# Last slot weights in a buffer part of their own, turned ahead of the last two experts; one cast of the slot outputs; output in eight transfers

## The chip, the cores and the metric

One core of one Trainium2 chip runs the whole program. The time is the device time of one execution in microseconds (us). An execution that was profiled has a span as well: from its first instruction to its last, as the trace shows it.

## What is computed

The first half is a linear attention with a decaying state over 4 batches, 8 heads, 768 steps and head width 48. Its output, seen as 3072 tokens of 384 values, goes into a soft mixture of experts: 8 experts with 4 slots each, so 32 slots.

```python
x = attn_out.transpose(0, 2, 1, 3).reshape(B * S, H * D)   # 3072 x 384
logits = x @ phi                                           # 3072 x 32
d = softmax of logits over the tokens;  slot_input = d.T @ x
for e in range(8):
    slot_out[e] = relu(slot_input[e] @ w1[e]) @ w2[e]      # 4x384, 384x1024, 1024x384
c = softmax of logits over the slots
out = c @ slot_out                                         # 3072x32 @ 32x384
```

The change touches only the end: the weights c of the last tokens ("slot weights"), the second product of the experts, and the product c @ slot_out with the transfers of its result.

## The kernel before, in words

The program is written as named tasks (`add(name, engines, function, ...)`), and the string `ORDER` (lines 9 to 32) lists the tasks in the order in which they are issued. Each engine works through its own instructions in that order; a word such as `ND3:ACT` puts a task on the named engine. Engines wait for each other through semaphores, which the framework sets from the tiles and the parts of tiles that instructions read and write. Tiles come from named pools and go back to them when their last task is issued.

Attention runs in 12 units, and behind each three units the logits of a batch are worked on. The token axis is cut into pieces: three batches whole (pieces 0 to 2), then batch 3 in a piece of four chunks of 128 tokens (piece 3) and one of two chunks (piece 4, the last). For a piece b, the slot weights go through these tasks:

- `LT`, `SU`, `LC`, `NM` (lines 670 to 710): logits, minus their maximum over the slots, exponential, sum and reciprocal, in the tile `Ls` (float32).
- `NB` (line 713): `Ls` times the reciprocal, written as bf16 into the tile `Lc`, on POOL for pieces 0 and 1 and on DVE (VectorE) otherwise.
- `ND` (line 725): a copy inside `Lc` that repeats part of each group of 32 columns; on POOL unless the word in `ORDER` says otherwise.
- `LX` (line 766): PE (TensorE) turns `Lc`, one 128x128 transpose per chunk, into a PSUM tile.
- `LE` (line 770, recorded at the helper's lines 358 for DVE and 360 for ACT): the turned weights go to `LexpT`, slots by tokens.

`Lc` and `Ls` have room for six chunks, and there is one tile of each (lines 169 and 171): pieces use chunk places 0 to 3 (piece 3) and 0 to 1 (piece 4), so piece 4 writes where piece 3 was.

The experts' weights are loaded by tasks `W0` to `W15`, issued from POOL's queue, with a cast to bf16 on the way (lines 784 to 787). The last one, for the second matrix of the last expert, is cut into `W15a`, `W15b` and `W15`: four, three and one of its eight blocks. The second product of experts 4 to 7 is done by `Q10` (experts 4 and 5, 16 products), `Q11` (expert 6, 8), `Q12`, `Q13` and `Q14` (expert 7; 4, 3 and 1 products, each behind the load of its own blocks), line 923. All add up in one PSUM bank, `SO` (half of the tile `Yb`). `F` words are products whose result nobody reads (line 862); `F19_2` stands between `LX3` and `Q11`.

Behind the last task come lines 930 to 957: `SO` is cast to bf16 into `so`, the left half by ACT (ScalarE) and the right half by DVE. Then 24 rows follow: row i is the product of every 24th column of `LexpT`, starting at i, with `so` (line 951), whose 128x384 result is copied from PSUM by ACT for even i and by DVE for odd i (lines 953 and 955). Row 0 alone is made in two halves, one copied by each engine. After 1, 3, 4, 4, 4, 4 and 4 rows SP issues a transfer to the output (line 957). Each partition's rows lie side by side in the output, so a transfer of n rows moves one run of n x 1536 bytes per partition. The results wait in tiles that are free by then: `vT_all`, four parts of `mix`, one of the `raw` pool, `AT_all`.

Of the kernel before, what the change touches and what calls it, by code (L numbers as in the profile page):

```python
# [26 lines left out]
RM2 NM1 XE100:ACT EX2 W13 W14 NB1 L3 AL2 ET2 YE11 AC1 ZT2 RM3 EE2 ZC3 EX3 SU2 F10a_3 X111 X110 XE111:ACT AL3 F11a_1  # L27
ET3 W15a ND1 XE110 EE3:ACT LB4 RM4 DP2 G1 DP3 AC2 EX4 G2 ET4 AL4 G3 G5 LC2 GS EE4 F12_3 DP4 AC3 ZT3 AC4 LX1 NM2 NB2
F13a_1 MG UN SU3 LC3 F14_6 H00 R00:DVE NM3 H01 R01 F15a_5 HT00 ND2 W15b HT01 HE00 F16a_1 Q00 HE01 Q01 H11 LX2 LE2
R11 F17_2 LT4 H10 NB3 LE1:ACT R10:DVE SU4 W15 LC4 F18_6 HT11 HT10 HE10 HE11:ACT NM4 Q10 ND3:ACT LX3 NB4 F19_2 Q11  # L30
Q12 ND4 LX4 Q13 LE3 LE4 Q14
"""


# [12 lines left out]
class _Plan:  # L47
# [7 lines left out]
    def buf(self, pool):  # L55
        return _Buf(pool)

    def add(self, name, engs, fn, deps=(), bufs=()):
        self.by[name] = _Task(name, engs, fn, list(deps), list(bufs))
# [23 lines left out]
def kernel(  # L83
# [12 lines left out]
    nc = tc.nc  # L96
    B, H, S, D = r.shape
    C = 128
    NS = S // C
    Nn, Dm = out.shape  # L100
    ES = moe_phi.shape[1]
    E = moe_w1.shape[0]
# [17 lines left out]
    f32 = mybir.dt.float32  # L120
# [6 lines left out]
    def O(ins):  # L127
        return tc.keep_in_program_order(ins)

    pe, dve, act, pool, sp = nc.tensor, nc.vector, nc.scalar, nc.gpsimd, nc.sync  # L130
# [18 lines left out]
    vT_all = big.tile([128, 3 * HW], bf, name="vT_all")  # L149
# [9 lines left out]
    SW = nQ * D  # L159
    S_t = [cst.tile([128, nQ, 2, D], bf, name=f"S{j}") for j in range(3)]  # L160
    Z_t = [cst.tile([128, nQ, 2, D], bf, name=f"Z{j}") for j in range(3)]
    XW = Dm + 8
    x_t = [cst.tile([128, NS, XW], bf, name=f"x{j}") for j in range(NX)]
# [3 lines left out]
    xT_t = [xT_all[:, CC * j:CC * (j + 1)] for j in range(NXT)]  # L167
    LexpT = cst.tile([128, Nn], bf, name="LexpT")
    Lc_t = [cst.tile([128, NS, 128], bf, name=f"Lc{j}") for j in range(1)]
    zc_t = [cst.tile([128, 2 * C], f32, name=f"zc{j}") for j in range(1)]  # L170
    Ls_t = [cst.tile([128, NS, ES], f32, name=f"Ls{j}") for j in range(1)]
    E_t = [cst.tile([128, 2 * C], bf, name=f"E{j}") for j in range(2)]
    ET_t = [cst.tile([128, 2 * C], bf, name=f"ET{j}") for j in range(2)]
# [9 lines left out]
    T_t = [psb.tile([128, 1024], bf, name=f"T{j}") for j in range(3)]  # L183
    Ab = psb.tile([128, 2, 512], f32, name="Ab")
    Yb = psb.tile([128, 2, 512], f32, name="Yb")
    Y_t = [Yb[:, j, :] for j in range(2)]
    Mb = psb.tile([128, 512], f32, name="Mb")
# [157 lines left out]
    def consts_d():  # L345
# [4 lines left out]

    L = _Plan(dict(raw=raw, ks=ks_t, vj=vj_t, kn=kn_t, vn=vn_t, AT=AT_t, prs=pr_t[0:1], prl=pr_t[1:2], dv=dv_t,
                   **{f"{x}T": t for x, t in turned.items()},
                   S=S_t, Z=Z_t, x=x_t, zc=zc_t, Lc=Lc_t, Ls=Ls_t, E=E_t, ET=ET_t, T=T_t, A=[Ab], Y=[Yb], M=[Mb], **{f"xT{j}": [t] for j, t in enumerate(xT_t)}))
    buf, add = L.buf, L.add

    def ev(t, dst, src):
# [47 lines left out]
    for m in range(NLD):  # L404
        lg = m % 2
        pb = TT["p", m] = buf("pr" + "sl"[lg])
        for nm in "krv":
            dstT = TT[nm, m] = buf(nm + "sl"[lg] + "T")
            P = P2 if nm == "v" else 128
            for h in range(1 + lg):  # L410
# [3 lines left out]
                def rv(kb=kr[nm, m], lg=lg, h=h):  # L414
                    return rows(*kb, J if lg else JH)[:, :, h * JH:(h + 1) * JH]
# [6 lines left out]
                else:  # L422
# [3 lines left out]
                    def f_src(t, rv=rv, src=src, tab=tab):  # L426
                        eng = dve if t.eng == "DVE" else pool
                        O(eng.tensor_mul(src.inst.rearrange("p (j e s) -> p e j s", j=JH, e=2)[:, :, :, 0:D], rv(), tab))  # L428
                    sd = f"S{nm}{m}{hx}"
                    add(sd, "DVE" if m == 0 else "POOL DVE" if m < 2 else "POOL", f_src,  # L430
# [35 lines left out]
    for n in range(NU):  # L466
# [51 lines left out]
        Smid = buf("Z")  # L518
        Snew = Sb[n] = buf("S") if ui < U3 - 1 else None
        dvb = buf("dv")  # L520
# [42 lines left out]
        def f_y(t, Yf=Yf, rT=rT, vn=vn, dvb=dvb, Sold=Sold, Smid=Smid, a=tuple(ATb), n=n):  # L563
# [11 lines left out]
            for x in range(PH):  # L575
                q, c = cell(n, x)
                if c:
                    S = (Sold, Smid)[x // nQ]
                    O(pe.matmul(y[:, x // nQ, q * P2:(q + 1) * P2], rT.inst[:, x, :],  # L579
# [33 lines left out]
    for b, (bt, c0, c1) in enumerate(pieces):  # L613
        xb = xB[bt]
        nc_ = c1 - c0
        last = b == NPC - 1
        ny = 2 if nc_ == NS else 1
        us = list(range(U3 * bt + c0 // CC, U3 * bt + c1 // CC))
        xTs = [xTB[i] for i in us]
        Lcb, Lsb, Eb, ETb = buf("Lc"), buf("Ls"), buf("E"), buf("ET")  # L620
        nm_o, nm_n = nm_t[(b + 1) % 2], nm_t[b % 2]
        rm, al, mx, sm = rm_t[b % 2], al_t[b % 2], mx_t[b % 2], sm_t[b % 2]

# [183 lines left out]
    SX, SO = Y_t[0], Y_t[1][:, 0:Dm]  # L807
# [4 lines left out]
    so = cst.tile([128, Dm], bf, name="so")  # L812
# [105 lines left out]
    for name, g, prod, deps in parts:  # L918
# [8 lines left out]
        qd = name  # L927

    L.run(ORDER)
    O(act.copy(so[:, 0:Dm // 2], SO[:, 0:Dm // 2]))  # L930
    O(dve.tensor_copy(so[:, Dm // 2:Dm], SO[:, Dm // 2:Dm]))


    out_v = out.rearrange("(p n) m -> p n m", n=nN)
    ob = [T_t[0][:].bitcast(f32), T_t[1][:].bitcast(f32), T_t[2][:].bitcast(f32), Mb[:], Ab[:, 0, :], SX]
    mf = mix[:].bitcast(f32)
    OW = 4 * Dm
    obuf = [vT_all[:].bitcast(f32)] + [mf[:, x * OW:(x + 1) * OW] for x in range(4)] + [
        L.pools["raw"][0], AT_all[:].rearrange("p a b -> p (a b)").bitcast(f32)]
    sizes = [1, 3, 4, 4, 4, 4, 4]  # L940
    i = 0
    for gi, sz in enumerate(sizes):
        o_s = obuf[gi][:, 0:sz * Dm].rearrange("p (n m) -> p n m", m=Dm)
# [44 lines left out]
```

## Time and profile before

| | |
|---|---|
| runs | 120.91, 120.58, 119.62 us; median 120.58 |
| the profiled execution | 119.91 us, of which the span is 118.1 us |
| busy over the span | PE 98.4, DVE 94.2, ACT 86.4, POOL 62.1 us |
| moved by DMA | 31.81 MB; HBM read 39.42 MB, written 4.72 MB |
| granted TensorE clock, mean | 0.972 |

Times in the views are counted from the start of the span. A row of the timeline gives start, duration, engine, line, operation, tiles with shapes, count, and in brackets the idle time ahead of it with what ended it. The chain of work that ended last gives start, duration and the engine and line that the end hung on at that time; "issue" there is time in which nothing visible was waited for. A row of a table of windows gives the busy time of the engines (with counts), then the granted TensorE clock, the busy share of the 16 DMA engines and the GB/s that they moved. PE's rows are its products, PEld's the loading of their weights, and a Q after an engine's name is its sequencer or queue.

### The profile page before, as it was taken

Reading aid. Unit: us, or ns where it says so; the run is one execution under the profiler, and the core shown is the slowest. Engines: PE = TensorE matmul, PEld = TensorE weight load, DVE = VectorE, ACT = ScalarE, POOL = GpSimd, SP = SyncE. Lnnn points to the kernel's source line nnn. Section 1 sums busy time; section 2 is a strip of 40 time slices with the busy share of each in tenths; the row PEclk is TensorE's granted clock in tenths of the full one; section 3 lists DMA queues with packets and bytes.
Section 4 is the critical chain, followed back from the end, with each engine's and each line's share of the span. In section 5 each row is a group of like instructions: output and inputs, shape, how many; then the busy total and the mean of one; then the engine's idle time right before and its main releaser. Section 6 shows DMA issues by size and latency. Waiting matters only on the chain.

```text
span 118.1 us, 3926 instructions
## 1 busy us (share of the span) xinstructions
PE 98.4 (83%) x1657; PEld 71.9 (61%) x1662; DVE 94.2 (80%) x181; ACT 86.4 (73%) x139; POOL 62.1 (53%) x81
## 2 busy tenths in 40 slices
PE   3999895999999899897999998999889887795000
PEld 0366674788888788686778877877543443463000
DVE  6798987798999999798999989999889426499000
ACT  5759994999999999698899979979951243296000
POOL 7605999999999989999989210000505000000000
PEclk9999999999999999999999999999999999999855
DMA  1999999999999999999999999999999997149993
GB/s 31 315 375 389 392 400 398 381 394 397 381 382 373 316 230 222 214 218 212 214 216 218 209 221 212 214 218 208 222 210 221 209 209 132 20 193 419 416 410 160
DMA packets 10697, 31.81 MB, mean 269 GB/s; under 512 B 1336, under 2 KB 4664, under 8 KB 10680
## 3 DMA queue, kind: packets, MB, share of 16 engines
q0 software_dynamic: 2592, 12.58, 52.1%
q1 hardware_dynamic: 7944, 18.93, 42.5%
q8 instruction: 13, 0.21, 0.7%
q10 hardware_dynamic: 144, 0.05, 0.2%
q14 instruction: 4, 0.03, 0.1%
HBM read 39.42 MB, written 4.72 MB: 374 GB/s over the span
## 4 chain that ended last, share of the span: by engine, by line
PE 44%; DVE 25%; ACT 9%; POOL 7%; issue 6%; ACTq 1%; DVEq 1%; POOLq 0%
PE T L437 9%; POOL mix L428 6%; DVE AT_all L512 5%; PE Ab L507 4%; PE Yb L573 3%; DVE mix L955 3%; PE Yb L923 3%; PE Yb L568 3%; PE Yb L579 2%; PE T L482 2%; PE T L596 2%; PE T L492 2%; PE Mb L530 2%; PE Mb L533 2%; DVE dv L556 2%
## 5 line engine op out<-in xcount | busy, mean ns | idle before, releaser
L428 POOL TENSOR_TENSOR mix<-raw,tabl 128x768 bf16<-128x768 f32 x15 | 28.0, 1878 | 5.5 <-ACT tabl L398 5.4
L512 DVE TENSOR_TENSOR AT_all<-Ab,mask 128x1024 bf16<-128x1024 f32 x24 | 29.3, 1219 | 1.1 <-PE Ab L507 0.5
L360 ACT COPY mix<-T 128x1024 bf16<-128x1024 bf16 x19 | 19.1, 1021 | 4.9 <-PE T L437 3.4
L437 PEld LDWEIGHTS <-mix 128*128 128x128 bf16 x192 | 12.3, 101 | 2.4 <-DVE mix L428 0.7
L556 DVE TENSOR_TENSOR dv<-vn,Mb 128x768 bf16<-128x768 bf16 x12 | 11.4, 946 | 1.4 <-PE Mb L546 1.1
L428 POOL TENSOR_TENSOR mix<-raw,tabs 128x768 bf16<-128x768 f32 x6 | 10.8, 1816 | 0.0
L360 ACT COPY vT_all<-T 96x1024 bf16<-96x1024 bf16 x10 | 10.2, 1021 | 0.6 <-PE T L437 0.4
L507 PE MATMUL Ab<-mix 64*128 64x128 bf16 x192 | 9.5, 218 | 1.2 <-ACT mix L360 1.0
L360 ACT COPY xT_all<-T 128x768 bf16<-128x768 bf16 (+1 forms) x12 | 9.3, 784 | 1.3 <-PE T L596 1.3
L360 ACT CAST x<-Yb 128x768 bf16<-128x768 f32 x12 | 9.7, 807 | 0.1
L437 PE MATMUL T<-turnl,mix 128*128 128x128 bf16 x128 | 9.6, 219 | 0.1
L725 POOL COPY Lc<-Lc 128x384 bf16<-128x384 bf16 (+1 forms) x4 | 1.8, 460 | 14.5 <-DVE Lc L713 14.5
L713 POOL TENSOR_TENSOR Lc<-Ls,sm 128x192 bf16<-128x192 f32 x2 | 1.0, 504 | 15.0 <-ACT E L691 14.5
L360 ACT COPY vn<-T 128x768 bf16<-128x768 bf16 x11 | 8.8, 814 | 0.0
L453 DVE TENSOR_TENSOR pr<-T,mix 128x1024 bf16<-128x1024 bf16 x12 | 8.0, 683 | 0.0
L507 PEld LDWEIGHTS <-mix 64*128 64x128 bf16 x192 | 5.8, 94 | 3.5 <-issue 0.7
L573 PEld LDWEIGHTS <-AT_all 128*128 128x128 bf16 x192 | 6.7, 96 | 1.7 <-issue 0.2
L540 DVE TENSOR_TENSOR Z<-Mb,wT 128x384 bf16<-128x384 f32 x12 | 6.6, 553 | 0.9 <-PE Mb L533 0.8
L360 ACT COPY kn<-T 128x768 bf16<-128x768 bf16 (+1 forms) x10 | 7.2, 721 | 0.2
L573 PE MATMUL Yb<-vn,AT_all 128*128 128x48 bf16 x192 | 6.9, 183 | 0.1
L419 POOL CAST vj<-raw 128x768 bf16<-128x768 f32 x8 | 6.6, 830 | 0.6 <-POOL phi_s L337 0.6
L437 PEld LDWEIGHTS <-vj 128*96 128x96 bf16 x96 | 6.3, 123 | 1.0 <-issue 0.4
(187 smaller groups left out, 241.3 us busy)
## 6 DMA issues: line engine op xcount, KB each, us to landing
raw<-in_moe_w_dram POOLq DMA_DIRECT2D x13, 768.0 KB, 14.6
raw<-in_k_dram SPq DMA_DIRECT2D x4, 768.0 KB, 12.3
raw<-in_r_dram SPq DMA_DIRECT2D x4, 768.0 KB, 11.6
raw<-in_v_dram SPq DMA_DIRECT2D x4, 768.0 KB, 12.4
out_dram<-mix SPq DMA_DIRECT2D x3, 768.0 KB, 4.9
raw<-in_k_dram SPq DMA_DIRECT2D x4, 384.0 KB, 10.7
raw<-in_r_dram SPq DMA_DIRECT2D x4, 384.0 KB, 10.3
raw<-in_v_dram SPq DMA_DIRECT2D x4, 384.0 KB, 10.4
```

The source lines that it names most:

```text
L360: O(act.copy(dst, src))
L419: O(act.copy(o, i_) if t.eng == "ACT" else pool.tensor_copy(o, i_))
L428: O(eng.tensor_mul(src.inst.rearrange("p (j e s) -> p e j s", j=JH, e=2)[:, :, :, 0:D], rv(), tab))
L437: O(pe.transpose(Tb.inst[0:P, jj * 128:(jj + 1) * 128], sv[:, jj, :], (turn, turnl)[lg][:]))
L453: O(dve.tensor_mul(cv(pb), tv(), cv(kT)))
L507: O(pe.matmul(Abf.inst[:, e, x * C:(x + 1) * C], kT.inst[s, g * nQ + x, :], rT.inst[s, g * nQ + x, :]))
L512: O(dve.tensor_mul(AT.inst[:], Abf.inst[:].rearrange("p e (g t) -> p e g t", g=nQ), mask[:, None, None, :].to_broadcast([128, 2, nQ, C])))
L540: O(dve.tensor_mul(Smid.inst[:], Mf.inst[:, 0:SW].rearrange("p (q d) -> p q d", q=nQ)[:, :, None, :].to_broadcast([128, nQ, 2, D]), wT[:, ...
L556: O(dve.tensor_mul(dvb.inst[:].rearrange("p g e d -> p (g e) d"), vn.inst[:].rearrange("p g e d -> p (g e) d"), Mf.inst[:, 448:448 + 2 * P ...
L568: O(pe.matmul(y[:, h, 0:Dm], ident[:], dvb.inst[:, h * nQ:(h + 1) * nQ].rearrange("p g e d -> p (g e d)"), start=True, stop=False, skip_gr ...
L573: O(pe.matmul(y[:, x // nQ, q * P2 + e * D:q * P2 + (e + 1) * D], a[x // nQ].inst[:, e, q, :], vn.inst[:, x, e, :], start=False, stop=(c = ...
L923: O(pe.matmul(SO[32 * z:32 * z + 32, :], hT[g].rearrange("p y c -> p (y c)")[:, c:c + 32], w2_of(g * EG + x)[:, y, :], start=(g == 0 and y ...
```

## The change

- The last piece takes its `Lc` and `Ls` from pools of their own, `Lcl` and `Lsl`, which are chunk places 4 and 5 of the same tiles.
- In `ORDER`, `NB4` and `ND4` move ahead of `Q10`, and `ND4` runs on DVE, where it was on POOL behind `Q12`; `LX4` moves from behind `Q12` to right behind `LX3`; `F19_2` is gone; `LE3` moves ahead of `Q13`, and `LE4` runs on ACT in place of DVE.
- One ACT instruction casts all of `so`.
- The output goes in eight transfers of 1, 2, 3, 4, 4, 4, 4 and 2 rows. The second waits in `vT_all` beside the first; those behind it use the tiles as before, one transfer later.

```diff
-R11 F17_2 LT4 H10 NB3 LE1:ACT R10:DVE SU4 W15 LC4 F18_6 HT11 HT10 HE10 HE11:ACT NM4 Q10 ND3:ACT LX3 NB4 F19_2 Q11
-Q12 ND4 LX4 Q13 LE3 LE4 Q14
+R11 F17_2 LT4 H10 NB3 LE1:ACT R10:DVE SU4 W15 LC4 F18_6 HT11 HT10 HE10 HE11:ACT NM4 NB4 ND4:DVE Q10 ND3:ACT LX3 LX4
+Q11 Q12 LE3 Q13 LE4:ACT Q14
...
-                   S=S_t, Z=Z_t, x=x_t, zc=zc_t, Lc=Lc_t, Ls=Ls_t, E=E_t, ET=ET_t, T=T_t, A=[Ab], Y=[Yb], M=[Mb], **{f"xT{j}": [t] for j, t in enumerate(xT_t)}))
+                   S=S_t, Z=Z_t, x=x_t, zc=zc_t, Lc=Lc_t, Lcl=[Lc_t[0][:, NS - 2:]], Lsl=[Ls_t[0][:, NS - 2:]], Ls=Ls_t, E=E_t, ET=ET_t, T=T_t, A=[Ab], Y=[Yb], M=[Mb], **{f"xT{j}": [t] for j, t in enumerate(xT_t)}))
...
-        Lcb, Lsb, Eb, ETb = buf("Lc"), buf("Ls"), buf("E"), buf("ET")
+        Lcb, Lsb, Eb, ETb = buf("Lcl" if last else "Lc"), buf("Lsl" if last else "Ls"), buf("E"), buf("ET")
...
     L.run(ORDER)
-    O(act.copy(so[:, 0:Dm // 2], SO[:, 0:Dm // 2]))
-    O(dve.tensor_copy(so[:, Dm // 2:Dm], SO[:, Dm // 2:Dm]))
+    O(act.copy(so[:], SO))
...
-    obuf = [vT_all[:].bitcast(f32)] + [mf[:, x * OW:(x + 1) * OW] for x in range(4)] + [
+    vf = vT_all[:].bitcast(f32)
+    obuf = [vf, vf[:, Dm:]] + [mf[:, x * OW:(x + 1) * OW] for x in range(4)] + [
         L.pools["raw"][0], AT_all[:].rearrange("p a b -> p (a b)").bitcast(f32)]
-    sizes = [1, 3, 4, 4, 4, 4, 4]
+    sizes = [1, 2, 3, 4, 4, 4, 4, 2]
```

## The prediction

> **What bounds the kernel now.** The views in the order in which I read them: the page, the chain of work that ended last, a table of windows over the end, then SP's timeline. The change sits in the last 18 us only, so the page serves for its slices.
>
> ```profile
> span 118.1 us, 3926 instructions
> GB/s 31 315 375 389 392 400 398 381 394 397 381 382 373 316 230 222 214 218 212 214 216 218 209 221 212 214 218 208 222 210 221 209 209 132 20 193 419 416 410 160
> ```
>
> A slice is 2.95 us. The weights stream in at some 215 GB/s until slice 34, one slice (20 GB/s) is nearly empty, and then the output leaves at over 400. The chain shows what the empty slice waits for:
>
> ```profile
> 100.29 0.33 PE T L766 x4
> 100.62 0.15 issue
> 100.77 0.67 PE Yb L923 x12
> 101.44 0.22 PE T L766 x2
> 101.65 0.40 PE Yb L923 x4
> 102.05 0.02 issue
> 102.07 0.33 ACT so L930
> 102.40 0.02 issue
> 102.42 0.37 DVE so L931
> ...
> 103.12 0.36 DVE vT_all L955
> 103.47 3.72 DVE mix L955 x8
> ```
>
> PE adds up the experts and turns weights between, the last product ends at 102.05, the two halves of the cast follow one another (DVE starts when ACT is done), and the right half of row 0 passes through DVE until 103.48. From there the chain names DVE's copies, but the windows show another bound:
>
> ```profile
> 101.00:101.40 0.40, 0.40 (x13) 0.08 (x6) 0.16 (x1) 0.00 (x0) 0.18 (x1) 1.00 0.20 29
> 101.40:104.40 3.00, 2.44 (x20) 1.75 (x17) 1.93 (x6) 1.60 (x5) 0.00 (x0) 1.00 0.00 0
> 104.40:105.00 0.60, 0.60 (x4) 0.37 (x3) 0.60 (x3) 0.60 (x3) 0.00 (x0) 1.00 0.89 325
> 105.00:105.40 0.40, 0.40 (x3) 0.24 (x3) 0.40 (x2) 0.40 (x2) 0.00 (x0) 1.00 0.02 4
> 105.40:107.00 1.60, 1.60 (x9) 1.09 (x8) 1.60 (x4) 1.60 (x5) 0.00 (x0) 1.00 1.06 426
> 107.00:116.50 9.50, 1.03 (x5) 0.39 (x3) 2.05 (x5) 1.25 (x3) 0.00 (x0) 0.73 0.99 404
> 116.50:118.10 1.60, 0.00 (x0) 0.00 (x0) 0.00 (x0) 0.00 (x0) 0.00 (x0) 0.50 0.00 0
> ```
>
> The last two numbers of a row are the share and the rate of the DMA engines. Nothing moves from 101.4 to 104.4; the first row of output goes from 104.4 to 105.0; 0.4 us are empty; then the engines are full until 116.5. Behind that stand 1.6 us of ending. So the end is: when the first byte leaves, plus 4.72 MB at the full rate, plus the holes. DVE and ACT are done by 109. SP's issues stand against it:
>
> ```profile
> 103.54 0.37 SPq L957 DMA_DIRECT2D out_dram<-vT_all  x1
> 104.56 3.43 SPq L957 DMA_DIRECT2D out_dram<-mix  x4
> ```
>
> From issue to the first byte: 103.54 to 104.40 and 104.56 to 105.40, about 0.85 us both times. The hole is there because the second issue had to wait for three rows while the first transfer, one row, was gone in 0.6 us.
>
> **Part 1: the last piece's own place, the earlier turning, F19_2 gone.**
>
> ```profile
> 90.32 1.06 POOL L786 DMA_DIRECT2D raw<-in_moe_w_dram  x2
> raw<-in_moe_w_dram POOLq DMA_DIRECT2D x1, 96.0 KB, 10.8
> 101.72 0.32 PE L923 MATMUL Yb<-raw,AT_all 128*32 128x384 bf16 x1
> 99.56 0.17 DVE L709 RECIPROCAL sm<-sm 128x2 f32<-128x2 f32 x1
> 100.60 0.23 DVE L713 TENSOR_TENSOR Lc<-Ls,sm 128x64 bf16<-128x64 f32 x1 [0.87 <-PE T L766]
> 100.74 0.42 DVE L358 COPY LexpT<-T 128x512 bf16<-128x512 bf16 x1
> 100.89 0.29 POOL L725 COPY Lc<-Lc 128x128 bf16<-128x128 bf16 x1 [9.52 <-DVE Lc L713]
> 99.30 0.41 ACT L360 COPY Lc<-Lc 128x256 bf16<-128x256 bf16 x1
> ```
>
> NB4 waited 0.87 us for LX3 to read the shared `Lc`; with its own chunk places it can start at 99.75, right behind the reciprocal. ND4 on DVE is not in the trace: POOL's copy of the same shape took 0.29, so I take 0.3 and bound it by 0.23 and 0.42, the DVE rows here. It is done near 100.3. LX4 then follows LX3, whose four turns end at 100.62, at no wait; its two turns add 0.16 at most there (0.33 for four), while the 0.15 of issue, where F19_2 stood, and LX4's 0.22 behind Q12 go. So PE would be done with Q11 to Q13 some 0.2 us sooner. Q14 does not: its block is the second of the two issues at 90.32, so issued at about 90.85, and 10.8 us later is 101.65; its product starts at 101.72. The DMA engines run until 101.4 for it. The weights' transfers, not PE, hold the last product, and nothing of this change reaches POOL's queue ahead of that issue. So I cost part 1 at **0**, bounded by 0.2 us of gain, if the landing were not what holds it, and by 0.2 of loss, if LX4's two turns and ND4's price both come at PE's cost. What covers it: LE3 (0.42 on DVE) and LE4 (256 columns on ACT, about 0.41 by the 256-column row) run by 101.6, ahead of the cast at 102.07. If ND4 came over 0.8 us late, LX4 would hold Q11 to Q14, which stand behind it on PE, past the landing; one for one from there.
>
> **Part 2: one cast.** Prices of ACT by width:
>
> ```profile
> 102.07 0.32 ACT L930 CAST so<-Yb 128x192 bf16<-128x192 f32 x1 [2.37 <-PE Yb L923]
> 103.44 0.48 ACT L953 COPY mix<-Mb 128x384 f32<-128x384 f32 x1 [0.40 <-PE Mb L951]
> L360 ACT CAST x<-Yb 128x768 bf16<-128x768 f32 x12 | 9.7, 807 | 0.1
> 102.44 0.24 PE L951 MATMUL T<-so,LexpT 128*128 128x192 bf16 x1 [0.41 <-ACT so L930]
> 103.08 0.33 PE L951 MATMUL Mb<-so,LexpT 128*128 128x384 bf16 x1
> 103.40 0.33 PE L951 MATMUL Yb<-so,LexpT 128*128 128x384 bf16 x1
> 102.72 0.32 ACT L953 COPY vT_all<-T 128x192 f32<-128x192 f32 x1 [0.33 <-PE T L951]
> 103.39 0.55 DVE L955 COPY mix<-T 128x384 f32<-128x384 f32 x1
> ```
>
> A cast of 192 columns takes 0.32 and one of 768 takes 0.81, so 384 columns take 0.48 (0.32 + 192/576 x 0.49), and the copy of 384 says 0.48 too. The cast ends at 102.07 + 0.48 = 102.55, where the two halves ended at 102.79: 0.24 sooner. But both halves of row 0 start from there. The left one, 0.28 from product to copy (102.44 to 102.72 today), reaches ACT at 102.88 instead of 102.72; ACT is then busy to 103.20. The right product stands 0.08 behind the left one on PE (half of 0.16: two products of 384 columns further on, from 103.08 to 103.40, is 0.16 each). It reaches DVE at 102.97, which ends at 103.33; SP issued 0.06 behind that copy, so at 103.39 instead of 103.54. **Gain 0.15**, between 0.04 (the right half's weight load in series, about 0.15 lost of it, less overlap) and 0.24 (the whole of the cast).
>
> **Part 3: 1, 2, 3, 4, 4, 4, 4, 2.** DVE's eight copies in 3.72 us make 0.465 each. Row 1 goes to DVE at 103.25, done at 103.80; row 2 to ACT at 103.20, done at 103.70. The second issue stands at 103.86, 0.70 sooner than today, its first byte at 103.86 + 0.85 = 104.71. The first transfer runs from 103.39 + 0.86 = 104.25 to 104.85. So the hole closes: **gain 0.40**. The second transfer, 393 KB at 407 GB/s, lasts until 105.82. The third needs rows 3 to 5: DVE's third copy from 103.25 ends at 103.25 + 2 x 0.465 + 0.55 = 104.73, issue at 104.79, first byte 105.64, 0.18 ahead of need. Then 576 KB last 1.45 us against 0.93 between issues, and the backlog only grows. The last transfer, two rows, stands in a full queue; that it is short saves nothing. Cost: an eighth transfer. The 404 and 426 GB/s rows hold four changes from one transfer to the next and no hole, so a boundary costs 0 when the next is queued. Runs of 3072 bytes per partition are not in the output's rows: between the one-row transfer's 325 GB/s and 407 for the rest, two such transfers (786 KB) lose 0 to 0.49 us; the 325 holds a start and an end within 0.6 us, so I take **0.05**, near the full rate.
>
> The Trainium skill, DMA: Bandwidth & Descriptors, section Anatomy of one DMA, fits a fixed cost of about 2.0 us per transfer plus its bytes at 436 GB/s (for transfers issued from GpSimd), and its section Bandwidth advises batches of 1 MiB or more. Paid in the queue, the eighth transfer would add 2.0 us, an estimate by that page of 122.1; the rows from 105.4 to 116.5, full across the boundaries, speak for its being latency beside other transfers.
>
> **Sum.** 0 - 0.15 - 0.40 + 0.05 = -0.50 us. Against the profiled execution: span 118.1 to 117.6, and its own time 119.91 to 119.4. That execution lies 0.67 below the median of the runs, so against the median 120.58 the forecast is **120.1**.
>
> **Rivals.**
> *The eighth transfer is paid (slower).* Place: the boundary of transfers 1 and 2 and that before the last. Mechanism: short transfers drain before the next one's first byte, and their runs go at the one-row rate. Then the hole of 0.40 stays, one more start of 0.85 lies open, 0.49 is lost on the rate, and 0.15 gained: 120.58 - 0.15 + 0.85 + 0.49 = 121.8. Only the first transfer is seen to drain, for which the second came 0.70 too late; against it stands the full stretch from 105.4. It decides as soon as the holes and lost rate exceed 0.55 us together. Chance 0.10.
> *The hole stays, the start moves.* The second issue depends on ACT and DVE both; if row 1's or 2's copy waits for something new (`vT_all` is shared with the transfer in flight), the issue slips by up to 0.5 and only 0.1 is left: 120.5. The copies' order is regular in the rows, which speaks against. Chance 0.13.
> *Q14 was not held by the landing.* If PE's queue was the limit, 0.2 more: 119.9. For it: the chain has the four last products as one row from 101.65, with no wait shown. Against it: the landing's sum, 101.65. Chance 0.15.
> *The forecast*, 120.1: chance 0.62.
>
> **How the numbers follow.** The runs before lie between 119.62 and 120.91, 1.1% apart, so a median of three cannot tell less than about 1% from no change. The forecast is 0.4% of gain. The cases but the slow one reach from 119.9 to 120.5, the bounds (0.2 by part 1, 0.1 by part 2, 0.44 by the rate) from 119.8 to 120.7; with half the spread of the runs on both sides I take 119.2 to 121.0, which leaves out the slow rival and a little below. Faster by over 1% (below 119.4) takes the third rival or the forecast with a low draw of the runs: 0.17. Slower by over 1% (above 121.8) takes most of the first rival, which lies at that edge: 0.08. Within 1%: 0.75.
>
> **What would show it.** Part 1: ND4 on DVE near 100.0 to 100.3, LX4 by 100.9, Q13 done by 101.5, PE idle, and Q14's product still at 101.7. Part 2: one cast of 0.48 ending at 102.55, first issue at 103.4. Part 3: second issue near 103.9, the DMA share above 0.9 from 104.4 on with no empty window, its end near 116.0. Wrong if Q14 starts before 101.5, if an empty window stands behind the first or second transfer, or if the DMA's full stretch is longer than 11.7 us.

## The result and the profile after

The changed kernel takes 119.87 us (median of 22 runs, 118.92 to 121.29) against 120.45 us for the kernel before (22 runs, 119.57 to 122.22). The ratio is 0.994, with a 95% interval of 0.9915 to 0.9964, that is 0.4 to 1.0 us faster. The profiled execution took 118.92 us with a span of 117.1 us. Ratios here and below leave out the executions that took over 1.5% more than the fastest of their kernel; the medians and ranges above include them.

The chain of work that ended last, for the changed kernel from the last weights on:

```profile
90.29 10.90 DMA raw<-in_moe_w_dram
101.18 0.04 issue
101.22 0.34 PE Yb L923
101.56 0.02 issue
101.58 0.49 ACT so L930
102.07 0.04 issue
102.11 0.26 PE T L951
102.37 0.02 issue
102.39 0.33 ACT vT_all L953
102.72 0.03 issue
102.75 0.55 DVE vT_all L955
```

What was hidden in the chain before is now written in it: the end hangs on the load of the last expert's last block. It lands at 101.18, PE starts the last product 0.04 later, and one cast of 0.48 stands where two stood in a row.

The timeline of the part that was reordered:

```profile
99.01 0.17 DVE L709 RECIPROCAL sm<-sm 128x2 f32<-128x2 f32 x1
99.21 0.22 DVE L713 TENSOR_TENSOR Lc<-Ls,sm 128x64 bf16<-128x64 f32 x1
99.47 0.20 DVE L358 COPY Lc<-Lc 128x128 bf16<-128x128 bf16 x1
99.67 0.51 PE L766 MATMUL T<-permT,Lc 128*128 128x128 bf16 x6
100.11 0.51 PE L923 MATMUL Yb<-tabl,AT_all 128*32 128x384 bf16 x8
100.22 0.37 ACT L360 COPY LexpT<-T 128x256 bf16<-128x256 bf16 x1 [1.11 <-PE T L766]
101.22 0.32 PE L923 MATMUL Yb<-raw,AT_all 128*32 128x384 bf16 x1
```

NB4 no longer waits, ND4 takes 0.20 on DVE, and LX3 and LX4 are one row of six turns. PE has done Q11 to Q13 by then; the last row is Q14, alone, behind the landing.

SP's issues and the windows of the changed kernel (the last two numbers are the DMA engines' busy share and GB/s):

```profile
102.90 0.93 SPq L957 DMA_DIRECT2D out_dram<-vT_all  x2
104.38 3.42 SPq L957 DMA_DIRECT2D out_dram<-mix  x4
```

```profile
100.90:103.75 2.85, 2.16 (x14) 1.50 (x11) 1.27 (x4) 1.75 (x5) 0.00 (x0) 1.00 0.03 6
103.75:104.35 0.60, 0.60 (x4) 0.36 (x3) 0.60 (x3) 0.60 (x3) 0.00 (x0) 1.00 0.91 328
104.35:104.80 0.45, 0.45 (x3) 0.28 (x3) 0.45 (x2) 0.45 (x2) 0.00 (x0) 1.00 1.04 410
104.80:107.00 2.20, 2.20 (x10) 1.44 (x10) 2.20 (x6) 2.20 (x6) 0.00 (x0) 1.00 1.02 408
107.00:115.50 8.50, 0.39 (x2) 0.00 (x0) 1.41 (x4) 0.61 (x2) 0.00 (x0) 0.65 1.00 405
115.50:117.10 1.60, 0.00 (x0) 0.00 (x0) 0.00 (x0) 0.00 (x0) 0.00 (x0) 0.50 0.00 0
```

The two issues of 102.90 lie 0.47 apart, and the empty window behind the first transfer is gone: 328, 410 and 408 GB/s follow one another. First to last byte takes 11.76 us, where it took 12.11.

The spans differ by 1.0 us, and half of it is not the change. The last weights land at 101.67 in the profile before and at 101.18 in this one, they were issued at 90.84 and 90.29, and everything ahead of that issue is the same work in the same order. Counted from that landing to the end of the span it is 16.46 us before and 15.92 after: 0.54 us for the change in these two executions.

### The profile page after: what moved, and what is told of

Same layout as the page of the kernel before. It is cut to its first block, busy times and chain, and to the rows that moved or that the text cites. A ratio compares the mean times of both kernels' runs of the same rounds, so it can differ in the third digit from the quotient of the medians.

```text
span 117.1 us, 3929 instructions
## 1 busy us (share of the span) xinstructions
PE 97.9 (84%) x1661; PEld 71.2 (61%) x1661; DVE 94.3 (81%) x180; ACT 86.8 (74%) x140; POOL 61.9 (53%) x80
## 4 chain that ended last, share of the span: by engine, by line
PE 38%; DVE 22%; DMA 9%; ACT 8%; POOL 7%; issue 6%; ACTq 1%; DVEq 1%; POOLq 0%
PE T L437 9%; DMA raw<-in_moe_w_dram 9%; POOL mix L428 5%; DVE AT_all L512 5%; PE Ab L507 4%; DVE mix L955 3%; PE Yb L573 3%; PE Yb L568 3%; PE Yb L579 2%; PE T L482 2%; PE T L596 2%; PE T L492 2%; PE Mb L530 2%; PE Mb L533 2%; DVE dv L556 2%
## 5 line engine op out<-in xcount | busy, mean ns | idle before, releaser
L437 PEld LDWEIGHTS <-mix 128*128 128x128 bf16 x192 | 11.9, 99 | 2.2 <-DVE mix L428 0.7
L428 POOL TENSOR_TENSOR mix<-raw,tabs 128x768 bf16<-128x768 f32 x6 | 10.8, 1823 | 0.0
L482 PE MATMUL T<-ident,mix 128*128 128x128 bf16 x80 | 6.1, 219 | 0.2
## 6 DMA issues: line engine op xcount, KB each, us to landing
raw<-in_moe_w_dram POOLq DMA_DIRECT2D x13, 768.0 KB, 13.9
raw<-in_r_dram SPq DMA_DIRECT2D x4, 768.0 KB, 11.6
raw<-in_v_dram SPq DMA_DIRECT2D x4, 768.0 KB, 12.4
```

What stands on the lines that cost most here:

```text
L437: O(pe.transpose(Tb.inst[0:P, jj * 128:(jj + 1) * 128], sv[:, jj, :], (turn, turnl)[lg][:]))
L482: O(pe.transpose(Tb.inst[:, x * 128:(x + 1) * 128], kT.inst[:, x, :], ident[:]))
```

## The experiments

Each was timed against the kernel before on the same chip. The table has, from the traces, the time from the issue of the last weights (the 96 KB load) to their landing, from the start of the cast to the first issue of output, from that to the second issue, from the first to the last byte of output, and from the landing of the weights to the end of the span. The profiles of e1 and e6 are left out of it: in them PE's granted clock was 0.5 from 103.9 to 107.3 us and from 104.4 to 107.8, while the rows were made; in e1 the second issue then came 1.25 us behind the first, where e9 with the same code has 1.02.

| run | ratio to before (95%) | weights land after | cast to 1st issue | 1st to 2nd issue | output bytes | landing to end |
|---|---|---|---|---|---|---|
| before | 1 | 10.8 | 1.47 | 1.02 | 12.11 | 16.46 |
| after | 0.994 (0.9915 to 0.9964) | 10.9 | 1.32 | 0.47 | 11.76 | 15.92 |
| e1, e9: old sizes | 0.9993 (0.9956 to 1.0029); 0.9982 (0.9944 to 1.002) | e9: 11.7 | 1.31 | 1.02 | 12.13 | 16.32 |
| e2: two casts | 0.9966 (0.993 to 1.0001) | 11.2 | 1.46 | 0.47 | 11.73 | 16.03 |
| e3: old order | 0.9928 (0.989 to 0.9966) | 11.6 | 1.31 | 0.47 | 11.74 | 15.87 |
| e4: after again | 0.9941 (0.9909 to 0.9973) | 11.0 | 1.32 | 0.47 | 12.11 | 16.27 |
| e5: Q14 freed, after | 0.9926 (0.9886 to 0.9967) | 11.8 | 1.31 | 0.47 | 11.70 | 15.43 |
| e6: Q14 freed, before | 0.9974 (0.9927 to 1.002) | | | | | |
| e7, e11: twelve transfers | 1.0005 (0.9967 to 1.0043); 0.9948 (0.9922 to 0.9974) | 12.9; 12.4 | 1.31 | 0.47 | 12.03; 12.02 | 15.92; 15.90 |
| e8: part 1 alone | 1.0035 (0.9996 to 1.0073) | 11.9 | 1.47 | 1.02 | 12.10 | 16.45 |
| e10: five transfers | 0.9916 (0.9882 to 0.995) | 12.0 | 1.31 | 0.47 | 11.76 | 15.59 |

**e1 and e9, the old sizes in the changed kernel.**

```diff
-    obuf = [vf, vf[:, Dm:]] + [mf[:, x * OW:(x + 1) * OW] for x in range(4)] + [
+    obuf = [vf] + [mf[:, x * OW:(x + 1) * OW] for x in range(4)] + [
-    sizes = [1, 2, 3, 4, 4, 4, 4, 2]
+    sizes = [1, 3, 4, 4, 4, 4, 4]
```

> The changed kernel with the output transfers of 1, 3, 4, 4, 4, 4, 4 rows put back; the order and the one cast stay. Theory (the closed hole is the larger share): the second transfer waits for three rows again, its issue comes about 0.95 us behind the first issue instead of 0.47, an empty stretch of about 0.4 us of the DMA engines stands behind the first transfer, and the stretch from first to last output byte is about 12.1 us instead of 11.75; the time is 0.35 to 0.45 us over the changed kernel, 0.2 under the kernel before. Rival (the eighth transfer is paid): seven transfers instead of eight make it 0.5 us or more faster than the changed kernel. Rival (the turning ahead of the last experts gave the gain): no difference from the changed kernel.

> The changed kernel with transfers of 1, 3, 4, 4, 4, 4, 4 rows once more, for a profile in which PE's clock does not fall in the last stage (in the first look it was granted 0.5 from 104.1 to about 107.5, so the rows came slower). Theory: second issue 1.02 us behind the first, an empty stretch of 0.3 to 0.4 us of the DMA engines, first to last byte 12.1 us, as in the kernel before. Rival: with the one cast the rows come sooner and no empty stretch is left.

With the old sizes put back the times are near those of the kernel before: 0.9993 and 0.9982, against 0.994. The intervals overlap, so by time alone this is a hint; but the four kernels with the old sizes (e1, e9, e8, e6) all lie at 0.997 or above, and those with first transfers of one and two rows at 0.9966 or below, but for one timing of e7. From landing to end, 0.40 of the 0.54 us are lost again (16.32). Windows and issues of e9:

```profile
104.55:105.20 0.65, 0.65 (x4) 0.42 (x3) 0.65 (x3) 0.65 (x3) 0.00 (x0) 1.00 0.83 303
105.20:105.60 0.40, 0.40 (x3) 0.23 (x3) 0.40 (x2) 0.40 (x3) 0.00 (x0) 1.00 0.20 81
105.60:107.00 1.40, 1.40 (x7) 0.90 (x7) 1.40 (x4) 1.40 (x5) 0.00 (x0) 1.00 0.99 398
```

```profile
103.69 0.37 SPq L957 DMA_DIRECT2D out_dram<-vT_all  x1
104.71 3.41 SPq L957 DMA_DIRECT2D out_dram<-mix  x4
```

The hole is back between 105.2 and 105.6, a fifth busy, and the bytes take 12.13 us. The rival of the eighth transfer, which had seven transfers faster, falls.

**e2, the two casts in the changed kernel.**

```diff
-    O(act.copy(so[:], SO))
+    O(act.copy(so[:, 0:Dm // 2], SO[:, 0:Dm // 2]))
+    O(dve.tensor_copy(so[:, Dm // 2:Dm], SO[:, Dm // 2:Dm]))
```

> The changed kernel with the cast in two halves put back, left on ACT and right on DVE. Theory: the halves run one behind the other (ACT 0.32, DVE 0.36 us), the first output transfer is issued 0.15 us later behind the last product than in the changed kernel (1.50 instead of 1.35 us behind the end of the last product), the rest of the end is the same; 0.15 us slower. Rival (one engine's wider cast costs what the wait saves): first issue within 0.05 us of the changed kernel's.

The chain of e2:

```profile
101.64 0.33 ACT so L930
101.97 0.02 issue
101.99 0.37 DVE so L931
102.36 0.04 issue
102.41 0.26 PE T L952
```

The halves follow one another again, and the first issue comes 1.46 behind the start of the cast instead of 1.32: 0.14 us, as expected. The time, 0.9966, lies 0.26% over the changed kernel's 0.994, with intervals that overlap; by itself it decides nothing, and what shows this term is the trace.

**e3 and e8, part 1 undone and part 1 alone.** e3 has the `ORDER` and the pools of before in the changed kernel; e8 has those of the change in the kernel before.

```diff
-R11 F17_2 LT4 H10 NB3 LE1:ACT R10:DVE SU4 W15 LC4 F18_6 HT11 HT10 HE10 HE11:ACT NM4 NB4 ND4:DVE Q10 ND3:ACT LX3 LX4
-Q11 Q12 LE3 Q13 LE4:ACT Q14
+R11 F17_2 LT4 H10 NB3 LE1:ACT R10:DVE SU4 W15 LC4 F18_6 HT11 HT10 HE10 HE11:ACT NM4 Q10 ND3:ACT LX3 NB4 F19_2 Q11
+Q12 ND4 LX4 Q13 LE3 LE4 Q14
...
-        Lcb, Lsb, Eb, ETb = buf("Lcl" if last else "Lc"), buf("Lsl" if last else "Ls"), buf("E"), buf("ET")
+        Lcb, Lsb, Eb, ETb = buf("Lc"), buf("Ls"), buf("E"), buf("ET")
```

> The changed kernel with the order of the tasks and the shared buffer of the last slot weights put back (NB4 behind LX3, ND4 on POOL, LX4 behind Q12, the filler F19_2, LE4 on DVE); one cast and eight transfers stay. Theory (the landing of the last weights holds the last product): the last product starts within 0.1 us of that landing in both, and everything behind it is the same; within 0.1 us of the changed kernel. Rival (PE's queue held the last product): it ends 0.2 us or more later behind the landing, and the time is 0.2 us or more over the changed kernel's.

> The kernel before with part 1 alone: the buffer part of the last slot weights and the new order of the tasks. Two casts and seven transfers as before. Theory: Q14 is held by the landing of its weights in both, so within 0.1 us of before. Rival (the gain comes from the turning ahead): 0.3 us or more faster than before.

With the old order the rest of the change is as fast (0.9928), and the new order alone gains nothing (1.0035, interval 0.9996 to 1.0073). PE in e3:

```profile
100.52 0.34 PE L923 MATMUL Yb<-raw,AT_all 128*32 128x384 bf16 x4
101.44 0.80 PE L923 MATMUL Yb<-raw,AT_all 128*32 128x384 bf16 x4 [0.37 <-DMA raw<-in_moe_w_dram]
```

Even with LX4's turns between Q12 and Q13, PE waits 0.37 us for the weights ahead of Q13, and 0.13 again ahead of Q14, which starts at 101.92 behind a landing at 101.87. The part that was thought to be covered by the landing is covered.

**e4, the changed kernel again.**

> The changed kernel once more. Every engine's work up to the last experts is in the order of before, so the time at which Q10 starts (99.45 us in the profile of before, 98.90 in that of after) should scatter by about half a microsecond between executions of either kernel. Theory: the difference of 0.5 us that lies ahead of Q10 between the two profiles is such scatter, and the end, counted from the landing of the last weights, is the same as in the first profile of the changed kernel within 0.1 us. Rival: Q10 starts at 98.9 here too, and at 99.4 in kernels with the old order only.

Its time is the same (0.9941), Q10 starts at 99.16 and the weights land at 101.51: between the two first profiles, so Q10's place is scatter. But the end is not the same within 0.1: the bytes take 12.11 us. Issues and windows of e4:

```profile
103.23 1.31 SPq L957 DMA_DIRECT2D out_dram<-vT_all  x2
```

```profile
104.10:104.60 0.50, 0.50 (x3) 0.30 (x2) 0.50 (x2) 0.50 (x2) 0.00 (x0) 1.00 0.97 344
104.60:105.00 0.40, 0.40 (x3) 0.30 (x2) 0.40 (x2) 0.40 (x2) 0.00 (x0) 1.00 0.18 58
105.00:105.40 0.40, 0.40 (x3) 0.30 (x2) 0.40 (x2) 0.40 (x2) 0.00 (x0) 1.00 0.95 361
```

The second issue came 0.47 behind the first, as ever, but the two took 1.31 us on SP where they took 0.93, and the second transfer's first byte came 1.34 us behind its issue. The hole was back in this one execution. In it a 16 KB packet of the instruction queue ran from 103.22 to 104.17, over the second issue; in the first profile of this kernel such a packet was over by 103.46. The shortest, median and longest issue of the two, in ns, for e3, the first profile and e4:

```profile
L957 SPq DMA_DIRECT2D out_dram<-vT_all x2: 369/370/372, 103.6 to 104.1; - x2
L957 SPq DMA_DIRECT2D out_dram<-vT_all x2: 370/412/454, 102.9 to 103.4; - x2
L957 SPq DMA_DIRECT2D out_dram<-vT_all x2: 369/603/837, 103.2 to 103.7; - x2
```

The first issue always takes 0.37 us. The second takes 0.37 too where the packet is over before it starts (e3, e5, e7, e11). Where the packet reaches into it, it ends 0.37 us behind the packet's end: in e2, e10 and the first profile, with an overlap of 0.04 to 0.09 us, and in e4, with 0.47. The eight profiles of these sizes agree in this, but no experiment moved the packet, and why the issue waits for it stays open.

**e5 and e6, the last product freed from the last landing.** In both kernels Q14 reads block 6 of the last expert's second matrix, so its result is another there.

```diff
-                            w2_of(g * EG + x)[:, y, :], start=(g == 0 and y == 0),
+                            w2_of(g * EG + x)[:, min(y, nF - 2) if g and x == 3 else y, :], start=(g == 0 and y == 0),
```

> The changed kernel, whose last product (Q14) reads block 6 of the last expert's second matrix in place of block 7; the load of block 7 is still made, but nothing computes with it, so this part of the result is another. This takes the last landing away from PE. Theory (the landing holds Q14, and PE's queue has room in the changed order): Q14 starts 0.35 to 0.45 us sooner, held now by the landing of blocks 4 to 6, and the time is 0.3 to 0.45 us under the changed kernel. Rival (PE's own queue sets Q14): no difference.

> The kernel before with the same edit: Q14 reads block 6 in place of block 7, whose load is made but not used. Theory (before, the landing and PE's queue ended within 0.05 us of each other, the turning LX4 standing ahead of Q13): Q14 starts at most 0.1 us sooner, the time within 0.1 us of before. So the new order would be worth 0.3 us or more where the landing does not cover it. Rival (the order is worth nothing even then): as much is gained here as in the changed kernel, 0.3 us or more.

In e5, Q13 and Q14 run as one row behind the load ahead of the last one, and the landing of the last block comes 0.43 us after Q14 has started:

```profile
101.91 0.35 PE L923 MATMUL Yb<-raw,AT_all 128*32 128x384 bf16 x4 [0.89 <-DMA raw<-in_moe_w_dram]
```

From that landing to the end it is 15.43 us instead of 15.92, so the landing holds Q14, and close to 0.5 us can be had there. The time moved by less than it can tell (0.9926 against 0.994). For e6 the expectation failed: there, too, Q14 started 0.43 us ahead of the last landing. PE's rows of e6, with the old order, ahead of the fall of its clock:

```profile
102.09 0.35 PE L923 MATMUL Yb<-raw,AT_all 128*32 128x384 bf16 x4 [1.35 <-DMA raw<-in_moe_w_dram]
103.51 0.35 PE L923 MATMUL Yb<-raw,AT_all 128*32 128x384 bf16 x4 [0.86 <-DMA raw<-in_moe_w_dram]
```

The weights came so late (13.9 us from issue) that PE's queue did not matter in the old order either. The profile of the kernel before, in which the landing came only just behind PE's queue, has the earliest landing of all (10.8 us). By these rows the new order would pay only where the weights land earlier than in any profile here; no run shows such a case, so what the order is worth by itself stays open.

**e7 and e11, twelve transfers.** Sizes 1, 2, 3 and nine times 2 rows, in halves of the same tiles.

> The changed kernel with twelve output transfers, of 1, 2, 3 and nine times 2 rows, in the same tiles. Theory (a transfer that is issued while others are queued costs nothing, and runs of 3072 bytes go at nearly the full rate): the stretch from the first to the last byte grows by 0.1 us at most per four transfers and by the rate of the shorter runs, 0.1 to 0.4 us in all; no empty stretch. Rival (each transfer pays a start of its own, 0.85 us, or the page's 2.0): four more transfers cost 3.4 or 8 us.

> The kernel with twelve transfers once more, since its time (0.65% over the changed kernel) and its trace (0.3 us longer from first to last byte, 0.25 us shorter behind the last landing) do not agree. Theory (four more transfers cost 0.3 us at most): ratio to before 0.993 to 0.998. Rival (they cost something that the end of the trace does not show): ratio 0.999 or more again.

The first timing, 1.0005, looked like a cost of 0.8 us; the second gave 0.9948. Their intervals barely overlap, and what moved the first is not known; their traces agree. The windows of e11:

```profile
105.20:117.20 12.00, 3.64 (x16) 2.09 (x14) 4.66 (x11) 3.86 (x9) 0.00 (x0) 0.81 1.01 393
117.20:118.50 1.30, 0.00 (x0) 0.00 (x0) 0.00 (x0) 0.00 (x0) 0.00 (x0) 0.50 0.00 0
```

Full throughout, at 393 GB/s instead of 405: four more transfers and shorter runs cost 0.26 to 0.27 us on 11.76, 0.07 each. The ending behind the last landing of output is 0.25 us shorter in both (0.96 instead of 1.21), so from the landing of the weights to the end nothing is lost. A start of 0.85 for each would have been 3.4 us, so in a full queue these stores pay no start of their own. The Trainium skill (DMA: Bandwidth & Descriptors, Anatomy of one DMA) fits a fixed cost of about 2.0 us to a transfer issued from GpSimd; paid in the queue by each of the four, it would be 8 us, an estimate by that page, which these traces do not bear out.

**e10, five transfers.**

```diff
-    obuf = [vf, vf[:, Dm:]] + [mf[:, x * OW:(x + 1) * OW] for x in range(4)] + [
-        L.pools["raw"][0], AT_all[:].rearrange("p a b -> p (a b)").bitcast(f32)]
+    obuf = [vf, vf[:, Dm:], AT_all[:].rearrange("p a b -> p (a b)").bitcast(f32), mf, mf[:, 8 * Dm:]]
-    sizes = [1, 2, 3, 4, 4, 4, 4, 2]
+    sizes = [1, 2, 5, 8, 8]
```

> The changed kernel with five output transfers, of 1, 2, 5, 8 and 8 rows (the five in the tile of the experts' hidden values, the eights in the two halves of the large tile). Theory (the queue is kept full by what is issued, not by the count of transfers): first issue as in the changed kernel, a hole of about 0.1 us ahead of the third transfer, whose five rows come 1.63 us behind the first issue, and shorter bookkeeping; first to last byte 11.7 us, and the end behind the last landing 0.3 us shorter, since SP waits for the transfers' semaphores in a fixed order at 0.06 us each and the last one here is late in it: 0.1 to 0.3 us under the changed kernel. Rival (large transfers come too late): a hole over 0.5 us ahead of the third or fourth, slower than the changed kernel.

```profile
106.10:106.40 0.30, 0.30 (x2) 0.17 (x2) 0.30 (x2) 0.30 (x1) 0.00 (x0) 1.00 0.44 179
106.40:116.30 9.90, 1.75 (x8) 0.89 (x6) 2.77 (x6) 1.97 (x5) 0.00 (x0) 0.77 0.98 412
116.30:117.50 1.20, 0.00 (x0) 0.00 (x0) 0.00 (x0) 0.00 (x0) 0.00 (x0) 0.50 0.00 0
```

The small hole ahead of the third transfer is there (0.44 busy in 0.3 us), the longer runs go at 412 GB/s, and behind the last byte stand 1.2 us instead of 1.6. From landing to end it is 15.59 us, 0.33 under the changed kernel, about what was expected; 0.31 of it lie behind the last landing of output (0.90 instead of 1.21), and the bytes take as long as in the changed kernel. By time it is the fastest of all (0.9916), but its interval overlaps that of the changed kernel.

## Why the prediction was right, step by step

- *Part 1 at 0*: right. The chain after names the load, e3 and e8 show no gain. There was luck in the reading: in the profile before, Q13's products started at 101.58 and the landing came 0.09 us later, the closest margin of all; in every other profile it comes 0.40 to 0.45 us behind Q13's start, and Q13 itself mostly waited for its own load (0.37 us in e3, 1.35 in e6). So the rival "Q14 was not held by the landing" was further off than its chance of 0.15. ND4 on DVE was priced 0.3 and took 0.20; LE4 at 0.41 took 0.37, the cast at 0.48 took 0.48.
- *Part 2, 0.15*: right. The cast to the first issue went from 1.47 to 1.32, and e2 gives 0.14 back.
- *Part 3, 0.40 less 0.05*: right in its sum, 0.35 (12.11 to 11.76), and in its mechanism in seven of the eight profiles with first transfers of one and two rows; in e4 the hole stayed and the sum was 0. Its two terms were each a little larger: the DMA engines' mean busy time went from 11.65 to 11.75 us, so the shorter runs and the eighth transfer cost 0.10 where 0.05 was put, and 0.45 of hole went.
- *What no term had*: behind the last landing of output the span ends 0.06 us sooner (1.21 instead of 1.27). At the end SP waits for the loads' and transfers' semaphores in one fixed order, about 0.06 us per wait, and the last transfer's place in that order has moved by one; in e10 it is last of its kind and 0.90 us are left.
- *The sum*, -0.50: from landing to end the two first traces have -0.54 and e4 has -0.19; the time has -0.7 with an interval from -1.0 to -0.4, which cannot tell the parts from each other. The 1.0 us between the two profiled spans would have misled: 0.49 of it is the landing of the weights.
- *The rival of the paid transfer* falls by e7 and e11 in the traces: no hole at any boundary of a filled queue. *The rival of the hole that stays* is wrong in its reason, since no copy waited for anything new, but e4 shows that the hole can come back in single executions, by a longer issue on SP.
- *Its signs of being wrong*: taken as written, all three came up, and two of them say nothing against the mechanism. Q14 started at 101.22, before the 101.5 named, but only because the landing came 0.49 us sooner; it still follows that landing by 0.04 us, and the sign should have been counted from there. The full stretch took 11.76 us, over the 11.7 named, but the prediction's own sum gives 11.76 (12.11 - 0.40 + 0.05). The empty window behind the first transfer is that of e4, and it does count: there part 3 gained nothing.
- *Its working*: the full rows from 105.4 to 116.5 hold five changes from one transfer to the next, not four, and half the spread of the runs on both sides of 119.8 and 120.7 would reach from 119.2 to 121.3, not to 121.0. Neither moves the forecast.

## What to carry to other kernels

Where a stage ends with output that fills the DMA engines, its end is the first byte plus the bytes at the full rate plus the holes; size the first transfers so that each lasts until the next one's first byte, here about 0.85 us behind its issue, and let the rest be large. Ahead of a reordering on an engine, ask what the last instruction of the sequence waits for: work moved out of the way of a product that a load holds gains nothing. Compare two profiles from a common event near the change, not from the start of the span.

## What the runs showed of the hardware that was not expected

- The same 96 KB load, behind the same queue of loads, landed 10.8 to 13.9 us after its issue, in executions whose work up to there is the same. That scatter is as large as that of the runs (118.9 to 121.3 us for the changed kernel), and larger than the whole change.
- SP's second output issue ended 0.37 us behind the end of a 16 KB packet of the instruction queue whenever the packet reached into it, in four profiles, and cost 0.47 us once (e4).
- With a full queue, a transfer of 128 runs of 3072 bytes costs little over its share of bytes: packets of 3072 bytes took 0.124 us against 0.239 for 6144.
